# Reciprocals of the softmax sums by block transposition and a DRAM scratch, and a shorter head, in a fused attention and two-layer MoE kernel

## The chip, the cores and the metric

One core of a Trainium2 chip runs the whole program: masked attention and then two dense feed-forward layers. The metric is the device time of one execution in microseconds (us); it is compared as the median of several runs. The core's engines work side by side, each through its own instructions in order: TensorE (PE in the rows, its weight loads PEld), VectorE (DVE), ScalarE (ACT), GpSimd (POOL), and SyncE (SP), which here only issues DMAs. A queue is named with a q: SPq is what SyncE issues, ACTq what ScalarE issues.

## The reference

`q`, `k`, `v` are 2 x 8 heads of 768 x 64. Each row of q and of k gets a bucket from six sign bits of its product with `proj` (64 x 6). Attention is kept where the buckets agree:

```python
q_bits = (einsum('bhsd,dk->bhsk', q, proj) > 0); k_bits = (einsum('bhsd,dk->bhsk', k, proj) > 0)
mask = q_bucket[:, :, :, None] == k_bucket[:, :, None, :]
scores = where(mask, scale * q @ k.T, -1e9)
attn = exp(scores - max(scores)); attn = attn / (sum(attn) + 1e-9)
x = (attn @ v), laid out as 1536 tokens x 512
x = relu(x @ w_in) ** 2 @ w_out          # 512 -> 2048 -> 512
out = silu(x @ w_in2) @ w_out2           # 512 -> 2048 -> 512
```

All of it is in float32 quality: the kernel splits every operand in a high and a low part and makes three products.

## The kernel before, in words

The 16 heads are 8 pairs. A pair has 12 steps of its own (three blocks of 128 query rows for each of four half heads), so the attention is a loop over `d`, written out in order by hand: a prologue from d = -5, 96 steps, and a tail. One step `d` makes, on TensorE: six 128x128 transpositions of exponentials (`transp`, twice three), four products with v (`av`) of exponentials that are two steps older, and the four score products of a later block (`score_mm`). Its scores are read in the next step: VectorE takes the row maximum (`row_max`, `row_live`), ScalarE the exponential (`score_exp`). Each transposed tile is copied by ScalarE as high part (`t_hi`, tile `th`) and VectorE subtracts for the low part (`t_lo`, tile `tl`). The transposed tiles use three PSUM buffers in turn (`ps_t`), the scores two (`ps_s`): the second transposition of step d+2 takes the buffer that the first of step d+1 had, and so waits for that one's `t_lo`.

Once a pair there is a long step (d = 5, 17, 29, ... 77). In it TensorE also makes the sign bits of a later pair (`bits_mm`, 12 products), VectorE compares them (`bits_cmp`, two halves of 48x384, with a `t_lo` between), and two DMAs place the twelve rows of the pair's first head into the tiles that the scores are made of: `qq` by the SyncE queue, `kk` by the ScalarE queue (`place_bits`). ScalarE issues that DMA before the next step's `t_hi`, SyncE issues it behind the load of `vr` of the same step (`load_v`). The scores of step d+2 are the first that read these rows, in their third and fourth product (those with 76 rows). VectorE also does the early weight conversion in these steps (`w_exp`, `w_sign`, `w_low`): one such instruction in d = 29 and 77, two in 17, 41, 53 and 65.

The softmax sums of a pair (128 x 12) are turned into a tile of reciprocals spread over the columns of the transposed result: VectorE takes the reciprocal (`norm_rows`, d0+2 with d0 the step after the pair's last), GpSimd spreads it to 128x768, TensorE transposes that in six pieces (`rb_mm`, in the long step d0+5; for the seventh pair in step 92), ScalarE copies the result out of PSUM (`x_norm`; for the seventh pair VectorE multiplies), and GpSimd multiplies and stores (`x_mul`, `x_put`, one step later). The last pair goes its own way.

In the prologue the bits of the very first head are made with small products (`first_bits_mm`, `first_bits_cmp`), those of the second are placed by two DMAs (`second_place`). Products on zeros (`warm_up`; table `WARM`) are put between them.

The two MoE layers follow; their order comes from a planner with costs (`Plan`), and the change does not touch them.

Of the kernel before, what the change touches and what calls it, by code (L numbers as in the profile page):

```python
# [31 lines left out]
WARM = {-5: 3, -4: 2, -3: 2, -2: 2, 0: 1, 1: 1}  # L32
# [412 lines left out]
def lsh_attention_moe_moe(ctx, tc, kd, qk, qf, fq, v, pc, wi1, wo1, wi2, wo2, out):  # L445
# [22 lines left out]
    ps_o = att.enter_context(tc.tile_pool(name="ps_o", bufs=1, space=PSUM))  # L468

# [57 lines left out]
    def bits_mm(p):  # L527
        t = pair[p]
        hp, lp = t["hp"], t["lp"]
        ops = [(w[:, 48 * i : 48 * i + 48], x) for i in range(2) for (w, x) in ((pjh, hp[i]), (pjl, hp[i]), (pjh, lp[:, i]))]  # L530
        s = ps_s.tile([128, 2, 512], F32, tag="s", name=f"bs{p}")[:, 0], ps_t.tile([128, 512], F32, tag="t", name=f"bt{p}")
        for z in range(2):
            for j, (w, x) in enumerate(ops):
                mm(s[z][0:48, 0:QW], w, x[:, z * QW : (z + 1) * QW], start=j == 0, stop=j == 5)  # L534
# [86 lines left out]
    def first_bits_mm(i, z, warm=0):  # L621
        o = first["bits", i, z] = ps_t.tile([128, 512], F32, tag="t", name=f"bf{i}{z}")
        ops = first_ops(0, z)[i]
        for n, (w, rows_, x) in enumerate(ops):
            mm(o[0:76, 0:QW], pjd[rows_, w, 0:76], x, start=n == 0, stop=n == len(ops) - 1)  # L625
            if n == 0:
                warm_up(warm)

    def first_bits_cmp(i, z):
        m = tm[1 + i][64:76]  # L630
        nc.vector.tensor_scalar(
            out=pair[0][("qq", "kk")[i]][0][64:76, 1, half(z)], in0=first["bits", i, z][64:76, 0:QW],
# [185 lines left out]

    def norm_rows(p):
        ri = sums[p]  # L820
# [4 lines left out]
    rows = {}  # L825

    def rb_mm(p):
        s = ps_s.tile([128, 2, 512], F32, tag="s", name=f"rb{p}")
        for c in range(6):
            o = s[:, c // 3, c % 3 * 128 : c % 3 * 128 + 128]  # L830
            nc.tensor.transpose(o, rows[p][:, c].rearrange("p h d -> p (h d)"), ident)  # L831
        return s
# [6 lines left out]
    def x_norm(s, p):  # L839
        ta = xs[p][0].rearrange("p (a b) -> p a b", a=2)  # L840
        if p < 6:
            nc.scalar.copy(out=rows[p].rearrange("p c h d -> p (c h d)").rearrange("p (a b) -> p a b", a=2), in_=s[:, :, 0:QW])
        else:
            nc.vector.tensor_tensor(out=x_rows(p).rearrange("p (a b) -> p a b", a=2), in0=s[:, :, 0:QW], in1=ta, op=ALU.mult)

    def x_mul(p):
        if p < 6:
            ta = xs[p][0]
            nc.gpsimd.tensor_tensor(out=ta if p < 4 else x_rows(p), in0=rows[p].rearrange("p c h d -> p (c h d)"), in1=ta, op=ALU.mult)
# [20 lines left out]
    extra = defaultdict(list)  # L870
# [27 lines left out]
    for p in range(NPAIR):  # L898
        d0 = 12 * (p + 1)
        at(d0 + (-3 if p < NPAIR - 1 else -4), norm_sums, p)  # L900
        at(d0 + (2 if p < NPAIR - 1 else -3), norm_rows, p)
# [28 lines left out]
    with tc.manual_schedule():  # L930
# [12 lines left out]
        make_identity(nc, ident)  # L943

# [34 lines left out]
        at(-1, second_place)  # L979
# [20 lines left out]
        for d in range(-5, G // 2 + 3):  # L1000
# [25 lines left out]
            more = extra.pop(d, [])  # L1026
            if ready and more and d not in long:
                score_exp(*ready, m)
# [99 lines left out]
```

## Time and profile before

| | us |
|---|---|
| median of 3 runs (741.33 to 741.73) | 741.59 |
| the profiled execution | 741.74 |
| its span | 740.0 |
| attention, prologue and tail | about 0 to 236 |
| the two MoE layers | about 236 to 740 |

In the profile's page a line of the first part gives busy time, share of the span and instructions of every engine. In the timeline a row is: start, duration, engine, source line, operation, written tile and read tiles, shapes, how many were merged (x6), and in brackets how long the engine had been idle before and who ended that. Rows of the chain of work that ended last are: start, duration, engine, tile, line. Rows of a table of stretches are: the stretch, its length, then busy time and instructions of each engine, the granted TensorE clock (1.00 is full), the share of the 16 DMA engines, GB/s. The granted clock is 1.00 in every stretch of this profile.

### The profile page before, as it was taken

The page shows a single profiled execution, that of the slowest core. Times are in us where ns is not written, and L with a number is a line of the kernel's source. Part 1 is how long each engine was busy: PE and PEld are TensorE (multiplying, and loading weights), DVE is VectorE, ACT ScalarE, POOL GpSimd, SP SyncE. Part 2 cuts the span into 40 slices and gives each one's busy share as a digit, 9 for nine tenths or more (in the row PEclk, how much of TensorE's full clock was granted, in tenths as well). Part 3 has the DMA queues.
Part 4 walks back from the last instruction along what each step waited for, and adds up shares of the span by engine and source line. Part 5 has one row for each costly group of instructions (what it writes and reads, how often), then busy time and mean ns, then how long its engine had stood idle before and what let it go on. Part 6 is the DMA issues. An engine that isn't in the chain of part 4 may idle for free.

```text
span 740.0 us, 10899 instructions
## 1 busy us (share of the span) xinstructions
PE 734.0 (99%) x3740; PEld 627.7 (85%) x3740; DVE 610.2 (82%) x1151; ACT 461.8 (62%) x866; POOL 249.6 (34%) x219
## 2 busy tenths in 40 slices
PE   9999999999999999999999999999999999999998
PEld 4899999999998888888888888888888888888887
DVE  6999999999999998887878896788888777776442
ACT  6898998998896882773566278366335525623510
POOL 7457477877684104103103103500330320230000
PEclk9999999999999999999999999999999999999999
DMA  6886886786462113311320220002123024010012
GB/s 177 205 179 156 182 184 168 164 184 150 112 158 61 57 58 113 113 59 57 114 86 19 96 86 28 29 29 85 58 100 128 30 78 150 1 58 1 1 71 100
DMA packets 27639, 71.87 MB, mean 97 GB/s; under 512 B 4184, under 2 KB 9048, under 8 KB 27584
## 3 DMA queue, kind: packets, MB, share of 16 engines
q1 hardware_dynamic: 24824, 64.52, 31.5%
q0 software_dynamic: 2160, 5.90, 3.7%
q10 hardware_dynamic: 600, 0.75, 0.4%
q8 instruction: 30, 0.49, 0.3%
q14 instruction: 25, 0.20, 0.1%
HBM read 49.80 MB, written 3.15 MB: 72 GB/s over the span
## 4 chain that ended last, share of the span: by engine, by line
PE 98%; DVE 1%; ACT 0%; issue 0%; ACTq 0%; DVEq 0%
PE bank L341 35%; PE bank L260 21%; PE bank L231 12%; PE s L741 9%; PE t L777 8%; PE o L801 4%; PE o L802 4%; PE warm L732 1%; PE bs L534 1%; PE bt L534 1%; PE rb L831 1%; ACT P L761 0%; DVE tl L788 0%; PE bs L641 0%; PE bf L625 0%
## 5 line engine op out<-in xcount | busy, mean ns | idle before, releaser
L160 POOL TENSOR_TENSOR wp<-wt,wp 128x512 fp32r<-128x512 f32 x56 | 78.2, 1407 | 329.6 <-ACT wp L158 307.5
L260 PE MATMUL bank<-xb,wp 128*128 128x512 f32 x480 | 110.1, 389 | 0.0
L788 DVE TENSOR_TENSOR tl<-t,th 128x384 fp32r<-128x384 f32 x192 | 104.9, 548 | 2.4 <-ACT th L782 2.2
L260 PEld LDWEIGHTS bank<-xb,wp 128*128 128x128 f32 x480 | 90.1, 188 | 18.7
L761 ACT ACTIVATE P<-s,mt 128x768 f32<-128x768 f32 x96 | 95.6, 996 | 11.8 <-DVE mt L753 7.2
L748 DVE TENSOR_REDUCE mt<-s 128x1 f32<-128x768 f32 x96 | 91.4, 952 | 4.9 <-PE s L741 4.2
L741 PE MATMUL s<-kk,qq 76*128 76x384 f32 (+1 forms) x384 | 84.6, 341 | 0.3 <-ACT P L761 0.2
L782 ACT CAST th<-t 128x384 fp32r<-128x384 f32 x192 | 82.3, 484 | 3.9 <-PE t L777 2.8
L158 ACT CAST wp<-wt 128x512 fp32r<-128x512 f32 x56 | 34.2, 619 | 78.2 <-DVE wt L215 44.5
L231 PE MATMUL bank<-x0h,wp 128*128 128x512 f32 x256 | 80.2, 389 | 0.0
L777 PE MATMUL t<-ident,P 128*128 128x128 f32 x576 | 79.3, 273 | 0.9 <-DVE tl L788 0.9
L777 PEld LDWEIGHTS t<-ident,P 128*128 128x128 f32 x576 | 67.8, 140 | 6.0 <-DVE tl L788 1.3
L801 PE MATMUL o<-th,vv 128*128 128x384 f32 x192 | 72.5, 378 | 0.0
L265 DVE TENSOR_TENSOR ts<-bank,ts 128x512 f32<-128x512 f32 x80 | 54.4, 690 | 19.9 <-PE bank L260 17.2
L741 PEld LDWEIGHTS s<-kk,qq 76*128 76x128 f32 (+1 forms) x384 | 67.9, 188 | 2.2 <-ACT P L761 1.0
L802 PE MATMUL o<-tl,vv 128*128 128x384 f32 x192 | 64.5, 336 | 0.3 <-DVE tl L788 0.3
L245 ACT ACTIVATE ts<-bank 128x512 f32<-128x512 f32 x48 | 28.6, 596 | 49.3 <-PE bank L260 28.8
L231 PEld LDWEIGHTS bank<-x0h,wp 128*128 128x128 f32 x256 | 48.0, 188 | 10.0
L160 DVE TENSOR_TENSOR gql<-ts,gqh 128x512 fp32r<-128x512 f32 x64 | 43.8, 703 | 8.9 <-ACT gqh L158 8.9
L173 ACT ACTIVATE wt<-raw 128x512 f32<-128x512 f32 x58 | 38.1, 670 | 20.3 <-POOL wp L160 17.6
L341 PE MATMUL bank<-wol,gqh 128*128 128x512 f32 (+1 forms) x132 | 50.5, 383 | 0.0
L341 PE MATMUL bank<-woh,gql 128*128 128x512 f32 (+1 forms) x132 | 50.5, 383 | 0.0
(185 smaller groups left out, 1634.1 us busy)
## 6 DMA issues: line engine op xcount, KB each, us to landing
raw<-in_dram SPq DMA_DIRECT2D x64, 512.0 KB
kk<-in_dram POOLq DMA_DIRECT2D x15, 384.0 KB, 5.8
qq<-hq SPq DMA_DIRECT2D x28, 192.0 KB
vr<-in_dram SPq DMA_DIRECT2D x8, 384.0 KB
ta<-ob SPq DMA_DIRECT2D x31, 96.0 KB
tb<-ob SPq DMA_DIRECT2D x31, 96.0 KB
out_dram<-ts SPq DMA_DIRECT2D x11, 256.0 KB
rq<-in_dram SPq DMA_DIRECT2D x7, 384.0 KB
```

The costliest lines, as they stand in the source:

```text
L160: add(("DVE", "POOL")[pool], l, lambda: eng.tensor_tensor(out=lo(), in0=src(), in1=hi().bitcast(F32), op=ALU.subtract), (*rk, *hk), lk, po ...
L231: mm(bank[b], w[:, x, op, sl], t["x0"][y][:, kt], start=kt == 0 and j == 0, stop=kt == 3 and j == 2)
L260: mm(bank[b], w[:, p, op, k * 128 : k * 128 + 128], x[:, q, xop, k], start=first and k == 0 and j == 0, stop=k == 1 and j == 2, skip_group ...
L341: mm(bank[b][:, 0:wd], x, y, start=i == 0 and n == 0, stop=i == FB - 1 and n == 2)
L741: mm(s[:, n, 0:QW], t["qq"][h][0:kk, ab, c0 : c0 + 128], t["kk"][h][0:kk, ab, n * QW : (n + 1) * QW], start=ab == 0, stop=ab == 1)
L748: nc.vector.tensor_reduce(out=m[:, 0:1], in_=s[:, :, 0:QW], op=ALU.max, axis=AX.XY, negate=True)
L761: nc.scalar.activation(out=e.rearrange("p (a b) -> p a b", a=2), in_=s[:, :, 0:QW], func=AF.Exp, scale=m[:, 1:2], bias=m[:, 2:3], accum_ou ...
L777: nc.tensor.transpose(t[:, j * 128 : (j + 1) * 128], P[u, j][:, kt * 128 : (kt + 1) * 128], ident)
L782: nc.scalar.copy(out=th, in_=PT[g][0][:, 0:QW])
L788: nc.vector.tensor_tensor(out=tl, in0=t[:, 0:QW], in1=th.bitcast(F32), op=ALU.subtract)
L801: mm(o[:, 0:QW], vv, th, start=kt == 0, stop=False)
L802: mm(o[:, 0:QW], vv, tl, start=False, stop=kt == KT - 1)
```

## The change

The reciprocals no longer go over TensorE. VectorE takes the reciprocal into columns 0 to 11 of a 128x32 tile and transposes that in 32x32 blocks; four DMAs of 12 rows each, issued by SyncE, write the four blocks into a 12x128 scratch in DRAM; two DMAs, issued two steps later, read it back, spread over 64 partitions each; GpSimd multiplies two steps after that. `norm_rows` moves from d0+2 into the long step d0+5 (step 86 for the seventh pair), ahead of the weight conversion there; `x_mul` and `x_put` move from d0+6 to d0+9 (90 for the seventh). The bits of a pair go into one PSUM buffer of the scores and are compared by one instruction of 48x768, behind both `t_lo`. The last pair keeps the old way.

In the head the fillers change: one instead of four between the first bits, none instead of three, two and two in d = -5, -3 and -2, seven instead of two in d = -4. The first bits of q are compared for columns 0 to 127 first and for the rest last. The products for the second head's bits are put in another order, and its bits are placed by halves, each half as soon as it is compared.

```diff
-WARM = {-5: 3, -4: 2, -3: 2, -2: 2, 0: 1, 1: 1}
+WARM = {-4: 7, 0: 1, 1: 1}
...
+    dr = att.enter_context(tc.tile_pool(name="dr", bufs=2, space=bass.MemoryType.DRAM))
...
-        s = ps_s.tile([128, 2, 512], F32, tag="s", name=f"bs{p}")[:, 0], ps_t.tile([128, 512], F32, tag="t", name=f"bt{p}")
+        s = ps_s.tile([128, 2, 512], F32, tag="s", name=f"bs{p}")
...
-    def bits_cmp(s, p, z):
-        if z == 0:
-            pair[p]["bt"] = a1.tile([128, S], F32R, tag="bt", name=f"bt{p}")
+    def bits_cmp(s, p):
+        pair[p]["bt"] = a1.tile([128, S], F32R, tag="bt", name=f"bt{p}")
         nc.vector.tensor_scalar(
-            out=pair[p]["bt"][0:48, z * QW : (z + 1) * QW],
-            in0=s[z][0:48, 0:QW],
+            out=pair[p]["bt"][0:48].rearrange("p (a b) -> p a b", a=2),
+            in0=s[0:48, :, 0:QW],
...
-            if n == 0:
-                warm_up(warm)
-
-    def first_bits_cmp(i, z):
+            if i + z + n == 0:
+                warm_up(1)
+
+    def first_bits_cmp(i, z, a=0, b=QW):
...
-        ops = [(64 - NBR * i, *x) for i in range(2) for x in first_ops(1, z)[i]]
+        ops = [(64 - NBR * i, *first_ops(1, z)[i][n]) for i, n in ((0, 0), (1, 0), (1, 1), (0, 1))]
...
-    def second_place():
+    def second_place(z):
...
-                out=pair[0][x][1][64 : 64 + NBR, 1, :].bitcast(F32), in_=first["bt"][NBR * n : NBR * n + NBR].bitcast(F32)
+                out=pair[0][x][1][64 : 64 + NBR, 1, half(z)].bitcast(F32), in_=first["bt"][NBR * n : NBR * n + NBR, half(z)].bitcast(F32)
...
     def norm_rows(p):
+        if p < NPAIR - 1:
+            nc.vector.reciprocal(out=rc[:, 0:12], in_=sums[p])
+            nc.vector.transpose(out=rt, in_=rc)
+            ris[p] = dr.tile([12, 128], F32, tag="ri", name=f"ri{p}")
+            for b in range(4):
+                nc.sync.dma_start(out=ris[p][:, 32 * b : 32 * b + 32], in_=rt[32 * b : 32 * b + 12])
+            return
...
-    def rb_mm(p):
...
-            nc.tensor.transpose(o, rows[p][:, c].rearrange("p h d -> p (h d)"), ident)
...
+    def spread(p):
+        rows[p] = w = a1.tile([128, 6, 2, 64], F32, tag="rw", name=f"rw{p}")
+        w = w.rearrange("p c h d -> p (c h d)")
+        r = ris[p].rearrange("(h c) t -> h (c t)", h=2)
+        for h in range(2):
+            nc.sync.dma_start(out=w[64 * h : 64 * h + 64], in_=r[h : h + 1].broadcast_to([64, S]))
...
-            k = d0 + (5 if p < NPAIR - 2 else 8)
-            extra[k].append((rb_mm, x_norm, p))
-            at(k + 1, x_mul, p)
-            at(k + 1, x_put, p)
+            k = d0 + 5 if d0 + 5 in long else d0 + 2
+            mid[k].append((norm_rows, (p,)))
+            at(k + 2, spread, p)
+            at(k + 4, x_mul, p)
+            at(k + 4, x_put, p)
...
-        first_bits_mm(0, 0, 2)
-        warm_up(1)
-        first_bits_mm(1, 0)
-        warm_up(1)
-        first_bits_mm(1, 1)
         for i, z in ((0, 0), (1, 0), (1, 1)):
-            first_bits_cmp(i, z)
+            first_bits_mm(i, z)
+        for i, z, a, b in ((0, 0, 0, 128), (1, 0, 0, QW), (1, 1, 0, QW), (0, 0, 128, QW)):
+            first_bits_cmp(i, z, a, b)
...
-        at(-1, second_place)
+            mid[z - 2].append((second_place, (z,)))
...
-                bits_cmp(t, long[d], 0)
                 t_lo(g + 1)
-                bits_cmp(t, long[d], 1)
-            for dve, t, p in held:
-                dve(t, p)
-            if ready and not more and d not in long:
+                bits_cmp(t, long[d])
+            elif ready:
                 score_exp(*ready, m)
```

## Rows read from the trace of the kernel before

**Rows 1.** The page's first part: busy time of every engine.

```profile
PE 734.0 (99%) x3740; PEld 627.7 (85%) x3740; DVE 610.2 (82%) x1151; ACT 461.8 (62%) x866; POOL 249.6 (34%) x219
```

**Rows 2.** The timeline of TensorE from the long step 17 on.

```profile
59.47 0.82 PE L831 MATMUL rb<-ident,rw 128*128 128x128 f32 x6
60.05 0.94 PE L741 MATMUL s<-kk,qq 128*128 128x384 f32 x4
...
62.90 0.82 PE L777 MATMUL t<-ident,P 128*128 128x128 f32 x6
...
64.25 0.86 PE L741 MATMUL s<-kk,qq 128*128 128x384 f32 x4
64.95 0.27 PE L777 MATMUL t<-ident,P 128*128 128x128 f32 x1
```

**Rows 3.** The timeline of VectorE in the same stretch.

```profile
57.75 0.68 DVE L708 SCALAR_TENSOR_TENSOR wi<-raw,wi 128x512 uint32<-128x512 uint32 x1
...
58.69 0.55 DVE L788 TENSOR_TENSOR tl<-t,th 128x384 fp32r<-128x384 f32 x1
59.15 0.66 DVE L540 TENSOR_SCALAR bt<-bs,tmt 48x384 fp32r<-48x384 f32 x1
...
60.20 0.66 DVE L540 TENSOR_SCALAR bt<-bt,tmt 48x384 fp32r<-48x384 f32 x1
...
62.23 0.56 DVE L788 TENSOR_TENSOR tl<-t,th 128x384 fp32r<-128x384 f32 x1
```

**Rows 4.** The timeline of ScalarE there: the DMA of the bits.

```profile
60.90 0.73 ACTq L661 DMA_DIRECT2D kk<-bt  x1
```

**Rows 5.** The timeline of the long steps 53 and 29.

```profile
144.91 0.56 DVE L788 TENSOR_TENSOR tl<-t,th 128x384 fp32r<-128x384 f32 x1
...
145.42 0.38 PE L777 MATMUL t<-ident,P 128*128 128x128 f32 x2
...
88.45 0.96 DVE L748 TENSOR_REDUCE mt<-s 128x1 f32<-128x768 f32 x1 [0.50 <-PE s L741]
```

**Rows 6.** The timeline of the SyncE queue in and after step 17.

```profile
57.19 0.59 SPq L670 DMA_DIRECT2D vr<-in_dram  x1
60.89 0.78 SPq L661 DMA_DIRECT2D qq<-bt  x1
61.73 1.67 SPq L489 DMA_DIRECT2D rk<-in_dram  x1
```

**Rows 7.** The table of stretches while those bits travel (the last columns count).

```profile
62.75:63.25 0.50, 0.50 (x6) 0.47 (x5) 0.20 (x2) 0.50 (x1) 0.50 (x1) 1.00 0.26 43
63.25:63.75 0.50, 0.50 (x7) 0.50 (x6) 0.50 (x1) 0.50 (x3) 0.50 (x1) 1.00 0.00 0
```

**Rows 8.** The timeline of steps 86 to 94.

```profile
216.84 0.22 DVE L821 RECIPROCAL sums<-sums 128x12 f32<-128x12 f32 x1
...
229.22 0.95 DVE L844 TENSOR_TENSOR ys<-rb,ta 128x768 f32<-128x768 f32 x1
...
229.36 1.93 POOL L696 TENSOR_SCALAR wt<-wt 128x512 f32<-128x512 f32 x1 [1.09 <-ACT wt L692]
...
231.56 0.91 DVE L700 TENSOR_SCALAR wt<-wt 128x512 uint32<-128x512 uint32 x1
```

**Rows 9.** The chain of work that ended last, in the first 25 us.

```profile
1.31 4.02 PE warm L732 x9
...
13.54 1.01 PE bs L641 x4
14.55 0.54 PE warm L732 x2
```

**Rows 10.** The timeline of the head.

```profile
9.62 0.83 ACT L608 CAST qq<-fr 128x768 fp32r<-128x768 f32 x1
...
11.44 0.99 ACT L761 ACTIVATE P<-s,mt 128x768 f32<-128x768 f32 x1 [0.99 <-PE s L741]
...
12.57 0.96 PE L741 MATMUL s<-kk,qq 128*128 128x384 f32 x4
```

More of the change, by code (lines that the diff above doesn't have):

```diff
@@ L625, in first_bits_mm @@
             mm(o[0:76, 0:QW], pjd[rows_, w, 0:76], x, start=n == 0, stop=n == len(ops) - 1)
-            if n == 0:
-                warm_up(warm)
-    def first_bits_cmp(i, z):
+            if i + z + n == 0:
+                warm_up(1)
+    def first_bits_cmp(i, z, a=0, b=QW):
         m = tm[1 + i][64:76]
         nc.vector.tensor_scalar(
-            out=pair[0][("qq", "kk")[i]][0][64:76, 1, half(z)], in0=first["bits", i, z][64:76, 0:QW],
+            out=pair[0][("qq", "kk")[i]][0][64:76, 1, half(z)][:, a:b], in0=first["bits", i, z][64:76, a:b],
             scalar1=m[:, 0:1], scalar2=m[:, 1:2], op0=ALU.is_gt, op1=ALU.mult,
@@ L817, in norm_sums @@
         nc.gpsimd.tensor_scalar(out=sums[p], in0=sums[p], scalar1=1e-9, scalar2=None, op0=ALU.add)
+    rc = ac.tile([128, 32], F32, name="rc")
+    rt = ac.tile([128, 32], F32, name="rt")
     def norm_rows(p):
+        if p < NPAIR - 1:
[5 more added lines that the diff above has]
+            return
         ri = sums[p]
@@ L823, in norm_rows @@
         nc.gpsimd.tensor_copy(out=w, in_=ri.rearrange("p (h c) -> p c h", h=2).unsqueeze(3).broadcast_to([128, 6, 2, 64]))
-    rows = {}
-    def rb_mm(p):
-        s = ps_s.tile([128, 2, 512], F32, tag="s", name=f"rb{p}")
-        for c in range(6):
-            o = s[:, c // 3, c % 3 * 128 : c % 3 * 128 + 128]
-            nc.tensor.transpose(o, rows[p][:, c].rearrange("p h d -> p (h d)"), ident)
-        return s
+    rows, ris = {}, {}
+    def spread(p):
[4 more added lines that the diff above has]
+            nc.sync.dma_start(out=w[64 * h : 64 * h + 64], in_=r[h : h + 1].broadcast_to([64, S]))
     def x_sum(p):
@@ L837, in x_sum @@
             nc.gpsimd.tensor_tensor(out=ta[r, z], in0=ta[r, z], in1=tb[r, z], op=ALU.add)
[L839 to L844, printed above, removed]
     def x_mul(p):
-        if p < 6:
-            ta = xs[p][0]
-            nc.gpsimd.tensor_tensor(out=ta if p < 4 else x_rows(p), in0=rows[p].rearrange("p c h d -> p (c h d)"), in1=ta, op=ALU.mult)
+        ta = xs[p][0]
+        nc.gpsimd.tensor_tensor(out=ta if p < 4 else x_rows(p), in0=rows[p].rearrange("p c h d -> p (c h d)"), in1=ta, op=ALU.mult)
     def x_rows(p):
@@ L900, in lsh_attention_moe_moe @@
         at(d0 + (-3 if p < NPAIR - 1 else -4), norm_sums, p)
-        at(d0 + (2 if p < NPAIR - 1 else -3), norm_rows, p)
+        if p == NPAIR - 1:
+            at(d0 - 3, norm_rows, p)
         at(d0 + (3 if p < NPAIR - 1 else 0), x_sum, p)
         if p < NPAIR - 1:
-            k = d0 + (5 if p < NPAIR - 2 else 8)
-            extra[k].append((rb_mm, x_norm, p))
-            at(k + 1, x_mul, p)
-            at(k + 1, x_put, p)
+            k = d0 + 5 if d0 + 5 in long else d0 + 2
[3 more added lines that the diff above has]
+            at(k + 4, x_put, p)
     for i, (d_load, d_abs, *d_dve) in enumerate(W_STEPS):
@@ L1025, in lsh_attention_moe_moe @@
                 t_hi(g + 1)
-            more = extra.pop(d, [])
-            if ready and more and d not in long:
-                score_exp(*ready, m)
             if d in long:
@@ L1037, in lsh_attention_moe_moe @@
                 t = bits_mm(long[d])
-            held = [(dve, pe(p), p) for pe, dve, p in more]
             if d in long:
-                bits_cmp(t, long[d], 0)
                 t_lo(g + 1)
-                bits_cmp(t, long[d], 1)
-            for dve, t, p in held:
-                dve(t, p)
-            if ready and not more and d not in long:
+                bits_cmp(t, long[d])
+            elif ready:
                 score_exp(*ready, m)
@@ L1061, in lsh_attention_moe_moe @@
         assert not new
-        assert not todo and not extra and not mid and not scale
+        assert not todo and not mid and not scale
         att.close()
```

6 lines of the change are left out of this document (3 added, 3 removed).

## The prediction

> **What bounds the kernel now.** I read the page's first part, then the chain of work that ended last, then the timelines of single long steps engine by engine, last the DMA traffic. The page shows TensorE busy for 734.0 of 740.0 us and VectorE for 610.2 [rows 1]; a busy TensorE says little by itself, so what counts is whether its groups follow each other. In a long step they do: transpositions of the reciprocals at 59.47, scores at 60.05, and a plain step later everything again, 64.25 to 64.95 for a group of four scores [rows 2]. So TensorE sets the pace, and what is taken off it is time saved, as long as nobody else becomes late. VectorE and ScalarE are close behind, so the question is who comes next. The head up to some 20 us is another thing: there the chain alternates between waits for exponentials and fillers that stand in TensorE's queue [rows 9, 10]. Everything after 236 us only moves with it.
>
> **What TensorE loses.** The six transpositions of a pair cost it 60.05 - 59.47 = 0.58 us [rows 2]; six pairs have them in a long step: 3.48 us, and the seventh 0.58 in step 92. Two other queues decide how much of that arrives.
>
> **VectorE in the long step.** Before: from the first `t_lo` at 58.69 to the end of the second compare, 60.20 + 0.66 = 60.86, it is 2.17 us [rows 3]. After: two `t_lo` at 0.46 (59.15 - 58.69) and one compare of 768 columns. That form is not in the trace. A 768-column operation on PSUM takes 0.95, the 384-column `t_lo` 0.55 [rows 3, 8], so 384 more columns cost 0.40, and the compare 0.66 + 0.40 = 1.06. Sum 1.98, a saving of 0.19. Added ahead of the weight conversion: the reciprocal 0.22 [rows 8], its hand-over 0.03 (the compare ends at 60.86, the DMA that waits for it starts at 60.89 [rows 3, 6]), and the 128x32 block transposition, which no row shows: at least nothing, at most the 0.66 of a compare with twelve times the columns; I take 0.22, the reciprocal's, which has the same partitions and is as small. That is 0.47 added, 0.28 net (0.06 to 0.72): the bits are compared 0.28 later, at 61.14. The Trainium skill (VectorE: DVE Perf Modes, "The three transpose paths") gives 0.311 us for a 128x128 bf16 transposition in 32x32 blocks; this would put ours below that, and the sum would change by less than 0.1 a pair. No row here shows it.
>
> Behind the compare stands ScalarE: it waits for it to issue the DMA of the kk bits (60.90, 0.73 [rows 4]), only then comes `t_hi` of the next step, then `t_lo`, which ends at 62.23 + 0.56 = 62.79 [rows 3]. The second transposition of step 19 needs that buffer; it starts half a group after 62.90, at 62.90 + 0.29 = 63.19 [rows 2]. The slack is 0.40 us. If TensorE comes 0.58 earlier and `t_lo` 0.28 later, the slack is overdrawn by 0.46, and 0.12 of the 0.58 stays. In step 53 `t_lo` ends at 145.47 and the transposition starts at 145.71 [rows 5]: slack 0.24, gain -0.04. Steps 17 and 41 are like the first, 53 and 65 like the second. In 29 and 77, with one conversion less, VectorE idles 0.50 before its next reduction [rows 5], which takes the 0.28; there some 0.5 stays. Sum over six: 0.24 - 0.08 + 1.0 = 1.2 us instead of 3.48.
>
> **The SyncE queue in the long step.** The four stores to the scratch are queued on SyncE ahead of the load of `vr` and of the qq bits. They wait for the block transposition: reciprocal from 57.75 [rows 3], 0.22 + 0.03 + 0.22 + 0.03, so the first is issued at 58.25. A DMA of twelve rows holds SyncE 0.78 and the next follows at 0.84 (60.89, 61.73), the 128-row load 0.59 [rows 6]. I take 0.84 for a store of twelve rows; lower bound 0.65 (the 128-row one with its gap), upper bound twice 0.84, since the next row shows 1.67 [rows 6]. Then `vr` is issued at 58.25 + 3.36 = 61.61 instead of 57.19 and the qq bits at 62.26 instead of 60.89, 1.37 late. Before, the traffic of the bits is over in the stretch that ends at 63.25 and nothing moves in the next [rows 7]: 2.36 us from issue to arrival. After: 62.26 + 2.36 = 64.62. The score group that needs them started at 64.25 [rows 2], and only its third product reads them, at 64.25 + 0.35 = 64.60. So the arrival falls on the old time, and the 0.58 is waited away, gain -0.02 a pair; with 0.65 a store it is 0.76 earlier, and VectorE's account above decides. If the 384 KB of `vr`, now right ahead in the same queue, delay them, it is worse; 0.1 us there is 0.6 over six pairs.
>
> The two accounts don't add; the later wait decides. For the six pairs I take 0.2 us, between -2.4 (0.4 worse each) and 1.2. The kk bits go over ScalarE's queue and are not behind the stores.
>
> **What lies beside other work.** ScalarE loses a 768-column copy a pair: it is not the bound there, nothing. GpSimd loses the spreading and multiplies three steps later, behind which only weight pieces for 236 us and the next casts stand: nothing, as long as it doesn't run over into the next long step. The two spreading loads a pair move 384 KB more; what waits for them is that multiplication alone: nothing.
>
> **Steps 86 to 94.** The reciprocal was there (216.84 [rows 8]); new is the transposition, 0.25 with its hand-over, in a step with one `t_lo` behind it: -0.25. In step 92 VectorE loses the 0.95 at 229.22 and TensorE 0.58, but VectorE's w_exp at 231.56 waits for GpSimd's 229.36 + 1.93 = 231.29 in any case [rows 8], so only about 0.2 comes through. Together about 0 (-0.3 to 0.6).
>
> **The head.** The first exponential starts at 11.44 [rows 10]. Ahead of it TensorE does four fillers between the first bits, of which one stays, and the first compare of q is cut to a third; so the first scores come over 1 us earlier. But ScalarE is busy till 9.62 + 0.83 = 10.45 with the second head's loads [rows 10], so the exponential starts at 10.46: 0.98 gained, and the score at 12.57 that waits for it comes at 11.59. The seven fillers fit in the wait: at 0.27 (0.54 / 2 [rows 9]) they take 1.9 at most, and the wait is about 1.6, so up to 0.3 of them may stick out. In the next two rounds a filler pair of 0.54 behind 1.01 of bits [rows 9] falls away; with that gone the loop of exponential, score and reduction limits, and I count half, 0.27 a round. Sum 0.98 + 0.54 = 1.5 us; bounds 0.7 (0.98 less what sticks out) and 2.06 (both pairs whole). The placement by halves must be done before step 1's scores; the halves are issued as much earlier as the scores are.
>
> **Sum.** 1.5 + 0.2 + 0 = 1.7. 741.74 of the profiled execution gives 740.04; it lies 0.15 above the median of the runs, so 739.9. About 0.2% (1.48 us) is what a measurement of this kernel can tell from no change: 740.11 and 743.07 are the borders.
>
> **The rivals.**
> Everything comes through: the stores are issued in 0.65 or less and the transposition costs next to nothing, or the slack is larger than I read. Then 1.5 + 3.48 + 0.58 = 5.6: 736.0. For it speaks that TensorE has no gap in these steps now; against it the 0.40 and 0.24 of slack and the twelve-row row of 0.78.
>
> Slower, by the SyncE queue alone: the qq bits arrive late for the third score product. From 0.25 us a pair later than before, the head's gain is gone; from 0.5 on it is slower by more than 0.2%. With 1.0 us a store (between 0.84 and 1.67) they are 0.64 later still: -0.66 x 6 + 1.5 = -2.5: 744.1. For it: 0.02 of reserve, and `vr` right ahead; against it: the queue is otherwise empty then [rows 7].
>
> The head gives little: the first exponential hangs on something else that doesn't move, such as the loads. Then 0.3 at most: 741.4. The clock is the other way to it: it is granted at 1.00, the 2.4 GHz level, in every stretch shown [rows 7], with fillers at 0.27 after the start against 0.45 in the first nine [rows 9]. If it fell in the two rounds from 12.6 to 17 for want of fillers, 0.70 + 1.01 of products a round would double: 3.4 lost, 0.98 kept, 743.8. Against it: the gaps left there are below 1 us. The Trainium skill (TensorE: Matmul & The Clock Gate, "What's actually happening") says that an idle TensorE drops to the lower clock, which speaks against taking fillers out; the rows show no drop, since the fillers are there.
>
> **Chances.** Forecast, 42%: own range 738.6 to 741.2 (head 0.7 to 2.06, pairs -0.3 to 1.0); more of it below 740.11 than above, 25 against 17. All through, 22%, all faster. Queue, 19%, of it 15 beyond 743.07 and 4 within. Head or clock, 17%: 13 within, 4 slower. Faster 0.47, same 0.34, slower 0.19. The range goes to 736.0, half of the second case, and to 743.0, where most of the third is left out.
>
> **What would show it.** In the pairs: an idle time of TensorE of about 0.5 us ahead of the third score product two steps after a long step, ended by the DMA of the qq bits; if it is instead ahead of a transposition, ended by `t_lo`, VectorE's account decided; if neither is there, all comes through. The store's issue time should be near 0.8 on SyncE, the block transposition near 0.2, the 48x768 compare 1.06. In the head: the first exponential at 10.5, the third score group at 11.6, the steady state 1.5 us earlier. Wrong it would be by a cheap store, by a `vr` that holds the bits back, by a clock below 1.00 in the first 20 us, or by a GpSimd queue that is late for the next bits.

## The result, and the profile after

The changed kernel takes 750.97 us (median of 4 runs, 750.14 to 751.59); the kernel before, beside it on the same chip, 741.46. The ratio is 1.0125 (95% interval 1.0113 to 1.0137): slower by 9.5 us, where 739.9 was forecast and 743.0 was the upper end. The profiled execution took 750.92, its span is 749.1.

The page's first part hardly tells of it. TensorE is busy for 0.6 us more than before [rows 1], VectorE for 1.4 more. The changed kernel:

```profile
PE 734.6 (98%) x3692; PEld 627.2 (84%) x3693; DVE 611.6 (82%) x1151; ACT 456.6 (61%) x860; POOL 246.8 (33%) x214
```

So I compared the starts of the score groups, one a step, in both timelines. The changed kernel is ahead by 1.84 us after the head, by 2.59 at the scores of step 53 (139.96 instead of 142.55), and behind by 3.71 at those of step 57 (154.59 instead of 150.88). Four steps lost 6.3 us. Till the last scores it falls back to 4.24 behind, till the first product of the MoE layers to 7.73 (243.57 instead of 235.84), and till the end to 9.18 (750.92 instead of 741.74). Two places, then: steps 54 to 57, and the end of the attention with what follows it at once (4.9 us).

The head went as forecast. The timeline of the changed kernel there: the first exponential starts at 10.58 instead of 11.44, the third score group at 11.71 instead of 12.57 [rows 10].

```profile
10.58 0.99 ACT L761 ACTIVATE P<-s,mt 128x768 f32<-128x768 f32 x1
...
11.71 0.98 PE L741 MATMUL s<-kk,qq 128*128 128x384 f32 x4
```

The first place, in the timelines of GpSimd, SyncE, VectorE and TensorE of the changed kernel:

```profile
125.31 1.84 POOL L853 TENSOR_TENSOR ta<-rw,ta 128x768 f32<-128x768 f32 x1 [4.82 <-DMA rw<-ri]
...
140.63 2.27 POOL L849 TENSOR_TENSOR ta<-ta,tb 128x768 f32<-128x768 f32 x1
...
136.52 0.46 SPq L814 DMA_DIRECT2D ta<-ob  x1
142.93 0.46 SPq L814 DMA_DIRECT2D tb<-ob  x1
143.48 2.14 SPq L829 DMA_DIRECT2D ri<-rt  x4
...
146.13 0.80 SPq L661 DMA_DIRECT2D qq<-bt  x1
...
138.24 0.22 DVE L825 RECIPROCAL rc<-sums 128x12 f32<-128x12 f32 x1
138.49 0.21 DVE L826 STREAM_TRANSPOSE rt<-rc 128x32 f32<-128x32 f32 x1
...
139.55 1.67 DVE L708 SCALAR_TENSOR_TENSOR wt<-raw,wt 128x512 uint32<-128x512 uint32 x1
...
142.07 1.06 DVE L540 TENSOR_SCALAR bt<-bs,tmt 48x768 fp32r<-48x768 f32 x1
...
141.75 0.55 PE L777 MATMUL t<-ident,P 128*128 128x128 f32 x3 [0.58 <-DVE tl L788]
...
149.16 0.59 PE L741 MATMUL s<-kk,qq 76*128 76x384 f32 x2 [2.45 <-DMA qq<-bt]
...
151.23 1.48 PE L741 MATMUL s<-kk,qq 128*128 128x384 f32 x4
```

Read it backwards. TensorE waits 2.45 us at 149.16 for the qq bits. SyncE issues these at 146.13, 3.0 us after the compare ended (142.07 + 1.06), because it stood at the copy into `tb` from 136.98 to 142.93, and what had queued behind that copy, the four stores (2.14 us) and `vr`, still came first. That copy may not overwrite `tb` before GpSimd has summed it, and the sum runs from 140.63 to 142.90. GpSimd has worked without a gap above 0.1 us since 125.31; ahead of that it waited 4.82 us for the spread reciprocals to land. The table of GpSimd's waits, from 30 to 245 us, has that for all pairs: 35.4 us together, more than GpSimd waits for anything else there.

```profile
POOL ta L853 <- DMA rw<-ri: 20.4, 4, 7.0
POOL ys L853 <- DMA rw<-ri: 15.0, 3, 5.5
```

There is a second, shorter way from the late GpSimd to TensorE. VectorE's two weight pieces of this long step took 0.89 and 1.67 us, at 138.62 and 139.55, while GpSimd's late product and sum ran beside them. Over all the kernels here, 143 pieces of this form ran in the attention with no GpSimd instruction beside them, and they took 0.65 to 0.69. The low part and the compare stand behind these pieces, and TensorE waits 0.58 at 141.75 for the low part and 0.20 at 143.19 for the compare. With the multiplication later (below) neither wait is there.

The four steps from 139.96 took 3.23, 3.01, 5.03 and 3.36 us, where the kernel before took 2.05 to 2.17. In the last one nothing is waited for; the products are slow (four scores in 1.48 instead of 0.87). The table of stretches gives the granted clock (the 1.00 and 0.66 behind the engines): after the wait TensorE spends part of the stretch at the lower of its two levels, 1.2 GHz.

```profile
145.00:150.00 5.00, 2.43 (x15) 2.11 (x16) 2.25 (x7) 2.94 (x7) 4.97 (x5) 1.00 0.60 151
150.00:155.00 5.00, 5.00 (x25) 4.91 (x24) 3.92 (x10) 3.33 (x7) 2.56 (x2) 0.66 1.22 216
...
240.00:245.00 5.00, 5.00 (x16) 4.23 (x17) 4.80 (x8) 0.47 (x1) 3.47 (x3) 0.50 0.02 7
```

The second place, timelines of GpSimd, VectorE and TensorE of the changed kernel:

```profile
212.82 1.85 POOL L853 TENSOR_TENSOR ys<-rw,ta 128x768 f32<-128x768 f32 x1 [5.47 <-DMA rw<-ri]
...
234.06 1.83 POOL L853 TENSOR_TENSOR ys<-rw,ta 128x768 f32<-128x768 f32 x1 [4.83 <-DMA rw<-ri]
235.97 0.24 POOL L817 TENSOR_SCALAR sums<-sums 128x12 f32<-128x12 f32 x1
236.29 1.93 POOL L696 TENSOR_SCALAR wt<-wt 128x512 f32<-128x512 f32 x1
...
236.25 0.23 DVE L832 RECIPROCAL sums<-sums 128x12 f32<-128x12 f32 x1 [1.78 <-POOL sums L817]
...
239.79 0.69 PE L802 MATMUL o<-tl,vv 128*128 128x384 f32 x1 [2.23 <-DVE tl L788]
```

Here the sixth and the seventh pair's multiplications wait 5.47 and 4.83 us. The last sums and the weight limits stand behind them in GpSimd's queue, VectorE waits for these twice (1.78, shown, and 1.36 at 238.25), its low part is late, TensorE waits 2.23, and from 240 to 245 it runs at the lower level throughout (0.50). In the kernel before the same weight limit was at 229.36 [rows 8].

### The profile page after: what moved, and what is told of

Its sections match the earlier page's. It is cut to its first block, busy times and chain, and to the rows that moved or that the text cites. A ratio compares the mean times of both kernels' runs of the same rounds, so it can differ in the third digit from the quotient of the medians.

```text
span 749.1 us, 10848 instructions
## 1 busy us (share of the span) xinstructions
PE 734.6 (98%) x3692; PEld 627.2 (84%) x3693; DVE 611.6 (82%) x1151; ACT 456.6 (61%) x860; POOL 246.8 (33%) x214
## 2 busy tenths in 40 slices
DMA packets 29478, 74.65 MB, mean 100 GB/s; under 512 B 5104, under 2 KB 10016, under 8 KB 29424
## 4 chain that ended last, share of the span: by engine, by line
PE 78%; DVE 13%; DMA 4%; POOL 2%; ACT 1%; issue 1%; SPq 1%; DVEq 0%; ACTq 0%; POOLq 0%
PE bank L341 35%; PE bank L260 20%; PE bank L231 12%; DVE mt L748 5%; DVE tl L788 5%; PE s L741 3%; PE t L777 3%; DMA rw<-ri 2%; PE o L802 2%; PE o L801 1%; PE warm L732 1%; DMA qq<-lp 1%; DVE bt L540 1%; DVE mt L753 1%; ACT P L761 1%
## 5 line engine op out<-in xcount | busy, mean ns | idle before, releaser
L777 PE MATMUL t<-ident,P 128*128 128x128 f32 x576 | 81.4, 275 | 3.7 <-DVE tl L788 3.6
L341 PE MATMUL bank<-woh,gqh 128*128 128x512 f32 (+1 forms) x132 | 50.5, 383 | 0.0
```

The costliest lines, as they stand in the source:

```text
L341: mm(bank[b][:, 0:wd], x, y, start=i == 0 and n == 0, stop=i == FB - 1 and n == 2)
L777: nc.tensor.transpose(t[:, j * 128 : (j + 1) * 128], P[u, j][:, kt * 128 : (kt + 1) * 128], ident)
```

## The experiments: where the loss comes from

Theories: **GpSimd** (the multiplication waits in an in-order queue), **SyncE** (stores ahead of the bits), **VectorE** (more work ahead of the compare), **head** (fewer fillers). Numbers of before are always those of the same chip.

**The reciprocals alone, on the head of before.** The edit puts back the fillers, the first compares and `second_place` of before.

> The head of the kernel before with the reciprocals of the changed one. Theory GpSimd (the multiplication waits in GpSimd's queue for the landing of the two spreading loads, what stands behind it comes late, and that costs 6.3 us in steps 54 to 57 and about 5 us at the end of the attention): the head has nothing to do with the loss and its 1.84 us come on top, 752.8 (752.0 to 753.6). Theories SyncE (the four stores stand ahead of vr and the qq bits) and VectorE (more work ahead of the compare): the same 752.8, since both lie in the reciprocals too. Theory head (the loss comes from taking fillers out, through a lower clock): 741 to 743.

Measured: 752.83 (before 742.03), ratio 1.0137 (1.0109 to 1.0164). As expected by the first three; the head is not the cause.

**The multiplication two steps later.**

```diff
-            at(k + 4, x_mul, p)
-            at(k + 4, x_put, p)
+            n = 6 if p < NPAIR - 2 else 4
+            at(k + n, x_mul, p)
+            at(k + n, x_put, p)
```

> The changed kernel with the multiplication and the stores behind it two steps later (d0+11 instead of d0+9) for the first six pairs; the seventh is left alone. Theory GpSimd: the loads have landed when GpSimd gets there, the 6.3 us of steps 54 to 57 are not lost, the 5 us at the end are: 744.7 (743 to 746.5). Theories SyncE and VectorE: nothing that they speak of is moved, 751 (750 to 752).

Measured: 740.53 (before 742.03), ratio 0.9986 (0.9972 to 1.0). All of the loss is gone, the end's too, which I had expected to stay. The timeline of GpSimd shows why: the sixth pair's multiplication now waits 1.77, and the seventh's 4.99 us fall early enough that nobody waits behind it. The profiled execution took 742.77, near the top of this kernel's range (739.36 to 742.88); in it TensorE waits 1.41 and 0.98 us for the qq bits after the long steps 17 and 65.

```profile
209.87 1.84 POOL L853 TENSOR_TENSOR ys<-rw,ta 128x768 f32<-128x768 f32 x1 [1.77 <-DMA rw<-ri]
...
227.57 1.83 POOL L853 TENSOR_TENSOR ys<-rw,ta 128x768 f32<-128x768 f32 x1 [4.99 <-DMA rw<-ri]
```

**The multiplication without the spread.**

```diff
-        ... in0=rows[p].rearrange("p c h d -> p (c h d)"), in1=ta, op=ALU.mult)
+        ... in0=ta, in1=ta, op=ALU.mult)
```

> The changed kernel, but GpSimd multiplies the sum by itself instead of by the spread reciprocals, so the normalisation of seven pairs is left out; all DMAs, the reciprocals and the multiplication's place and length stay. Theory GpSimd: both losses go, 739.6 (738 to 742). Theories SyncE and VectorE: stores, compare and reciprocals are all there, 751 (750 to 752).

Measured: 741.18 (before 742.03), ratio 0.9989 (0.998 to 0.9999). With stores, loads and reciprocals in place and only the wait taken out, the loss is gone: SyncE and VectorE are not its cause by themselves.

**The stores behind vr and the bits.**

```diff
             mid[k].append((norm_rows, (p,)))
+            last[k].append((norm_store, (p,)))
```

> The changed kernel with the four stores of a long step issued by SyncE behind vr and the qq bits instead of ahead of them. Theory SyncE: the bits arrive as early as in the kernel before, the 6.3 us of steps 54 to 57 are not lost, 744.7 or less. Theory GpSimd: the queue's head is held by the copy into tb, which waits for the sum on GpSimd, and that stands ahead of all of these, so at most 1 us is gained: 750 (749.5 to 751.5). Theory VectorE: 751.

Measured: 748.52 (before 742.03), ratio 1.0087 (1.0065 to 1.011). Outside both ranges and between them: 6.5 us are left of the 9.5, so behind the held copy the stores cost about 3 us (1 to 5 by the two intervals; 3.5 in the traces at step 57, where this kernel is 0.25 behind instead of 3.71). The theory GpSimd had allowed them 1 us at most. SyncE's timeline of this kernel shows both. The copy into `tb` still stands till 143.02, and the bits follow 1.2 later instead of 3.2; TensorE's wait is 1.73 instead of 2.45. The profile names no releaser for it, but it ends 3.1 us after the issue of the bits, as in the changed kernel (3.0).

```profile
143.02 0.46 SPq L814 DMA_DIRECT2D tb<-ob  x1
...
144.21 0.78 SPq L661 DMA_DIRECT2D qq<-bt  x1
145.04 1.73 SPq L836 DMA_DIRECT2D ri<-rt  x4
...
147.29 0.59 PE L741 MATMUL s<-kk,qq 76*128 76x384 f32 x2 [1.73 <-issue]
```

**Two buffers for tb.** `("tb", 1)` becomes `("tb", 2)`, and `rc`, `rt` become columns of `pcr`.

> The changed kernel with two buffers for tb instead of one (room for it is made by putting the two small tiles of the reciprocals into columns of a tile that is done with by then; the fill with ones falls away, the columns transposed for nothing hold other finite numbers). The multiplication still waits in GpSimd's queue as before. Theory GpSimd through tb (GpSimd's lateness reaches TensorE because the sum is late, so the one tb is not free, so SyncE stands at the copy into tb with vr and the bits behind it): SyncE is not held, the 6.3 us of steps 54 to 57 are not lost, at the end some is: 743 to 746. Rival (lateness reaches TensorE by another way, such as VectorE slowed beside GpSimd or the casts of v): 749 to 751.

Measured: 743.6 (before 741.82), ratio 1.0022 (1.0013 to 1.0032), in the range of the theory. GpSimd still waits 28.3 us for the spread in this kernel, but SyncE's timeline has the copy into `tb` at 136.91 and the bits as soon as they are compared. The single `tb` is the main link between GpSimd and TensorE in steps 54 to 57. What is still lost there in this trace (2.67 ahead at step 52, 1.91 at step 57) goes the shorter way: the two weight pieces took 1.09 and 0.99 beside GpSimd. The profiled execution took 741.48, the lowest of ten, and shows no loss at the end of the attention (11.48 us from the last scores to the MoE layers); where the 1.8 us of the median lie is not shown.

```profile
136.91 0.59 SPq L814 DMA_DIRECT2D tb<-ob  x1
...
141.81 0.80 SPq L661 DMA_DIRECT2D qq<-bt  x1
```

**One pair's multiplication later**, `n = 6 if p == 2 else 4`, and another kernel with `p == 5`.

> The changed kernel, the multiplication two steps later for the third pair alone (step 47 instead of 45). After its wait of 4.8 us ahead of that multiplication GpSimd works without a gap for 27 us, and the late sum of the fourth pair, which holds tb, is in that stretch. Theory that this one wait makes the 6.3 us of steps 54 to 57: they go, the end's 5 us stay, 744.7 (743 to 746). Theory that the lateness adds up from pair to pair: at most a third of it goes, 749 or more.

> The changed kernel, the multiplication two steps later for the sixth pair alone (step 83 instead of 81). Theory that its wait of 5.5 us makes the end late (sum of the seventh pair, copy into tb, spreading loads, second wait of 4.8 us, then the last sums and the weight limits): the end's 5 us go, the 6.3 of steps 54 to 57 stay, 746 (745 to 747.5). Theory that the seventh pair's own wait makes it: 751.

Measured: 746.33, ratio 1.006 (1.0046 to 1.0075), for the third pair; 745.79, ratio 1.0057 (1.0044 to 1.007), for the sixth (before 741.55). In the third pair's trace the lead is 0.80 before the long step and 0.78 after step 57: that loss is gone. The median is 0.3 above the range. This execution has a lead of 1.60 at step 53 where the changed kernel had 2.59, and 0.8 of the 6.3 is the rise at step 53 itself, which is given back without any wait for GpSimd too (0.79 in the kernel without the spread). VectorE's weight piece ran with no GpSimd instruction beside it in that step:

```profile
140.31 0.69 DVE L708 SCALAR_TENSOR_TENSOR wt<-raw,wt 128x512 uint32<-128x512 uint32 x1
```

The same trace has a new loss in steps 78 to 80 (from 1.27 ahead at step 77 to 0.99 behind; the changed kernel loses 0.5 there), where the piece at 194.82 took 2.16 beside the sum at 194.56. In the sixth pair's trace steps 54 to 57 still cost 7.7 (from 2.59 ahead to 5.11 behind), and the stretch from the last scores to the MoE layers is no longer than before (11.45 us, before 11.6, in the changed kernel 15.1). Each place hangs on one pair's wait.

**One step later instead of two**, `n = 5`.

> The changed kernel, the multiplication one step later instead of two for the first six pairs: of the 4.4 to 4.8 us between issue and landing one step of 2.05 more lies ahead of it. Theory of a queue with some reserve: waits of 2 to 3 us are borne, 741 (740.3 to 742.5). Theory that every us of wait counts: about half of the 10 us that two steps gave, 745 to 746.

Measured: 740.63 (before 741.55), ratio 0.9988 (0.9979 to 0.9997). GpSimd bears the waits that are left (up to 3.4 us in the first four pairs, 4.7 in the last three): they cost nothing that can be measured, those of the changed kernel 10 us. The length of a wait alone doesn't decide. In the changed kernel the fourth pair's multiplication, at 159.67, waits longest, 7.04 us, and TensorE loses nothing by it: it is 3.72 behind at step 58 and 3.73 at step 76. What counts is what stands behind the wait, and when it is needed.

## The experiments: what the long step gives when GpSimd is out of the way

With the multiplication later, 1.0 to 1.5 us are left of the head's gain and nothing of six times 0.58. These kernels ask why.

**The head alone**, reciprocals as before.

> The kernel before with the head of the changed one, reciprocals as before. Theory that the head's gain arrives whole: 1.85 us at the seventh score and no wait afterwards gives it back, 739.9 with before at 741.75 (739.4 to 740.3). Rival: the long steps, which run without a gap before, are brought out of step and give part back: 740.5 to 741.2.

Measured: 740.25 (before 741.66), ratio 0.9984 (0.9975 to 0.9993): 1.2 to 1.4 us. In its trace the lead is 1.13 after the head and 1.06 at the last scores, so nothing is given back; this execution's head gained less than the 1.84 above. Over all kernels with this head it is 1.1 to 2.1.

**Multiplication later and stores last, both.**

> Both edits at once: the multiplication two steps later and the four stores behind vr and the qq bits. With the multiplication later, the qq bits still made TensorE wait 1.0 us once (step 44) and the low part of a transposed tile 1.4 us in three long steps. Theory that SyncE's stores are a second, smaller cause, after GpSimd's wait: 1.0 us less than with the multiplication later alone, 739.5 (738.9 to 740.2; before at 742.0 on that chip, so about 2.5 below before). Theory that the stores cost nothing of their own: 740.5, as with the multiplication later alone.

Measured: 740.58 (before 741.82), ratio 0.9984 (0.9975 to 0.9993). No more than the later multiplication alone: that the stores cost something of their own, once the multiplication is later, is not shown. The wait of 1.0 us at step 44 that the expectation names is not in the trace of the later multiplication; its waits for the bits are the two given above. The table of TensorE's waits of this kernel, from 17 us on:

```profile
PE t L777 <- DVE tl L788: 2.6, 5, 0.9
PE s L741 <- DMA kk<-bt: 0.9, 1, 0.9
```

The low part takes the place of the bits, by the chain of the prediction. In step 17 (timelines of ScalarE, VectorE and TensorE) ScalarE waits for the compare (58.60 to 59.66), issues the kk bits at 59.69, starts the high part at 60.52; the low part waits for that 0.20, the second transposition 0.30:

```profile
59.69 0.73 ACTq L661 DMA_DIRECT2D kk<-bt  x1
60.52 0.86 ACT L782 CAST th<-t 128x384 fp32r<-128x384 f32 x2 [2.20 <-DVE mt L748]
...
61.03 0.56 DVE L788 TENSOR_TENSOR tl<-t,th 128x384 fp32r<-128x384 f32 x1 [0.20 <-ACT th L782]
...
61.65 0.55 PE L777 MATMUL t<-ident,P 128*128 128x128 f32 x3 [0.30 <-DVE tl L788]
```

**The compare in halves again**, with the multiplication later: `bits_mm` and `bits_cmp` as before, a `t_lo` between.

> The multiplication two steps later, and the bits again in two PSUM tiles, compared in two halves with the low part between them, as in the kernel before. With the whole compare, TensorE waits 0.2 to 0.6 us for the low part in three of the long steps and steps after. Theory that the whole compare behind both low parts makes this: the waits shrink, 739.5. Theory that the reciprocal and the transposition ahead of it make it, and the whole compare with its 1.06 instead of 1.32 is a help: the same or up to 1.5 slower than the 740.5 of the multiplication later alone.

Measured: 741.71 (before 741.82), ratio 1.0006 (0.9996 to 1.0017). About 1.5 worse than whole, with intervals that overlap by a little: the one compare is no cause of the loss, rather a help.

**Reciprocal and transposition behind the compare.**

```diff
-            mid[k].append((norm_rows, (p,)))
+            (behind if k in long else mid)[k].append((norm_rows, (p,)))
...
                 bits_cmp(t, long[d])
+                for fn, a in behind.pop(d, []):
+                    fn(*a)
```

> The kernel with multiplication later and stores last, and the reciprocal and the transposition in a long step behind the compare instead of ahead of the weight conversion. Theory chain: the compare ends 0.43 earlier, so the high part too; the low part stands behind the same VectorE work and gains only the 0.2 that it waited for the high part: five times 0.2, 739.6. Rival, what counts is the work on VectorE in that step and not its order: 740.6.

Measured: 739.93 (before 741.66), ratio 0.9976 (0.9967 to 0.9985). 0.6 better than with both edits, a little less than the chain's five times 0.2; the intervals overlap, so the size is uncertain.

**The kk bits by SyncE.** `(nc.scalar if n and not h else nc.sync)` becomes `nc.sync`.

> The kernel with multiplication later and stores last, and the kk bits of a pair's first head issued by SyncE behind the qq bits instead of by ScalarE. There TensorE still waits 0.3 to 0.9 us for the low part of a transposed tile in five of the long steps and steps after, 2.6 us in all. Theory (chain of the prediction: whole compare, ScalarE's issue of the kk bits, high part, low part, transposition): ScalarE no longer waits for the compare, these waits shrink to less than half, 739.2 or less with 740.6 for the kernel with both edits. Rival, VectorE has no room left whatever stands ahead of it: the same waits, 740.6. Rival, the kk bits come 0.8 later on SyncE and are waited for: 741 or more.

Measured: 740.41 (before 741.66), ratio 0.9988 (0.9979 to 0.9997). No faster than with both edits (0.9984). Its table of TensorE's waits shows the chain cut, and another wait, for a DMA that also queues on SyncE, in its place:

```profile
PE s L741 <- DMA kk<-lp: 1.0, 1, 1.0
...
PE t L777 <- DVE tl L788: 0.3, 1, 0.3
```

**Both orders.**

> All four edits: multiplication two steps later, stores last, reciprocal and transposition behind the compare, kk bits by SyncE. Theory that the low part's wait and the order on VectorE were all that kept the 0.58 of each long step back: 738.0 (737.3 to 738.8 with before at 741.7). Rival, another wait takes their place (the kk bits or the low half of k, which then queue on SyncE): 739.9, no better than with the order on VectorE alone.

Measured: 740.88 (before 741.55), ratio 0.9993 (0.9983 to 1.0002); its runs lie between 739.2 and 743.1. The rival holds: TensorE waits 0.7 for the low half of k and 0.5 for the qq bits, and in the median nothing is won.

**The reciprocals early, out of the long step**: `norm_rows` at d0-1, `spread` at d0+1, `x_mul` at d0+6.

> The changed kernel with the reciprocals early: reciprocal, transposition and stores at step d0-1 (two steps after the last exponential of the pair, six ahead of the long step), the spreading loads at d0+1, the multiplication at d0+6 as in the kernel before (d0+5 for the seventh pair). Theory GpSimd first, SyncE and VectorE in the long step behind it: all three go, since five steps lie between load and multiplication and the long step holds no reciprocal and no store; the head's 1.84 and most of six times 0.58 arrive: 737.5 (736 to 739.5). Rival, VectorE's whole compare is what is late in the long step: the waits of 0.2 to 0.6 for the low part stay, 740. Rival, VectorE has no room for 0.43 us at d0-1: seven times 0.4 lost there, 740 to 741.

Measured: 743.23 (before 741.82), ratio 1.002 (1.0011 to 1.0029). Wrong, by the second rival and one more. The long steps do keep 0.33 to 0.43 each; the loss lies outside them. The plain step has no room: the lead falls by 0.35 from the scores of steps 11, 23, 35 and 47 to the next. And at step 59 the reciprocal itself waits for the sums, which GpSimd adds to behind its other work (timelines of VectorE and TensorE of this kernel):

```profile
155.05 0.23 DVE L825 RECIPROCAL rc<-sums 128x12 f32<-128x12 f32 x1 [1.35 <-POOL sums L817]
...
156.02 0.55 PE L777 MATMUL t<-ident,P 128*128 128x128 f32 x3 [1.56 <-DVE tl L788]
```

**No transposition on VectorE, one DMA that puts each element by itself.**

```diff
+        nc.sync.dma_start(out=ris[p].rearrange("c t -> t c"), in_=sums[p])
```

> The changed kernel without the block transposition: the reciprocal is taken at d0+2 as in the kernel before (at d0-1 for the seventh pair), and one DMA writes the 128x12 tile into the 12x128 scratch with every element put by itself, 1536 pieces of four bytes; spreading at d0+7, multiplication at d0+11 (d0+2 and d0+5 for the seventh). Theory that the 0.43 us on VectorE in the long step and what SyncE issues there are what is left of the loss: the waits for the low part and for the bits go, head and six times 0.5 arrive, 737.5 (736.5 to 738.5). Rival, 1536 pieces hold the DMA engines and other transfers come late: 741 or more. Rival, the whole compare alone keeps the low part late: 740.

Measured: 781.98 (before 741.66), ratio 1.0558 (1.0541 to 1.0575). TensorE waits 28.2 us for the kk bits, in six places, and the granted clock is 0.976 over the execution. The rival of the 1,536 pieces holds: from 56 to 64 us the DMA engines are busy for 0.92 and then 0.73 of the time while they move only 54 and 30 GB/s; between 64 and 68 us they are busy throughout (1.01) and TensorE for 0.69 of 4 us:

```profile
67.31 0.98 PE L741 MATMUL s<-kk,qq 76*128 76x384 f32 x2 [4.53 <-DMA kk<-bt]
...
64.00:68.00 4.00, 0.69 (x2) 0.71 (x3) 0.00 (x0) 0.02 (x1) 0.88 (x2) 0.78 1.01 216
```

**One store for the four**, on the kernel with reciprocal and transposition behind the compare; and the same with the kk bits by SyncE.

```diff
-        for b in range(4):
-            nc.sync.dma_start(out=ris[p][:, 32 * b : 32 * b + 32], in_=rt[32 * b : 32 * b + 12])
+        nc.sync.dma_start(out=ris[p].rearrange("c (b t) -> b c t", b=4), in_=rt)
```

> The kernel with multiplication later, stores last, reciprocal and transposition behind the compare, and one DMA that stores all four blocks (128 pieces of 128 bytes, into a 32x128 scratch of which twelve rows are used) instead of four of twelve rows. SyncE is held some 0.5 instead of 1.6 to 2.1 us there. Theory that SyncE's queue is what is left: 739.2 (738.6 to 739.7, before at 741.6). Rival, the waits left have nothing to do with SyncE: 739.9, as with four stores.

> The same with the kk bits issued by SyncE as well, so that ScalarE doesn't wait for the compare. Theory that SyncE's queue took back what this edit gave with four stores (740.9 there): now it comes through, 738.3 (737.5 to 739.2). Rival, the bits wait for something else than SyncE: 740 to 741, and executions 2 to 3 us apart as with four stores.

Measured (before 741.8): 739.84, ratio 0.9973 (0.9962 to 0.9984); with the kk bits by SyncE 738.66, ratio 0.9958 (0.9945 to 0.9971). One store by itself changes nothing, as its rival has it. With it the other edit comes through, as the theory of the queue has it: without it that edit gave 0.9993. This is the best version found, 0.42% below before. Its step 17, ScalarE and SyncE: the high part starts at 59.39 and waits for no compare; SyncE issues both bits and the store within 2.3 us.

```profile
59.39 0.86 ACT L782 CAST th<-t 128x384 fp32r<-128x384 f32 x2 [1.08 <-PE t L777]
...
59.40 0.78 SPq L661 DMA_DIRECT2D qq<-bt  x1
60.22 0.77 SPq L661 DMA_DIRECT2D kk<-bt  x1
61.09 0.58 SPq L835 DMA_DIRECT2D ri<-rt  x1
```

## Why the prediction was wrong, step by step

**The step that failed** is in the part on what lies beside other work. It priced GpSimd's later multiplication at nothing, "as long as it doesn't run over into the next long step", and the two spreading loads at nothing because what waits for them "is that multiplication alone". It counted the multiplication's 1.8 us and not the wait ahead of it, and with that wait GpSimd did run over: it was still busy at 140.63, in the long step 53. In an in-order queue whoever stands behind a waiting instruction waits too: casts, weight pieces, and the sum that frees `tb`, for which SyncE waits, behind which stand `vr` and the bits. From the first issue of the two loads to the multiplication's start it is 4.9 us in the first and 4.2 in the seventh pair (rows of SyncE and GpSimd below; the seventh multiplication is at 234.06, above) and 9.6 in the fourth, against the two steps, 4.1 us, that the change leaves, and the loads are issued at the end of a step, late when SyncE is. The trace of before has no such load, and I gave it no bounds. All this is shown by the later multiplication and by the multiplication without the spread; the link through `tb` by the second buffer. The shorter way, over VectorE's slower weight pieces, is read from the traces side by side and has no experiment of its own.

```profile
65.52 1.24 SPq L844 DMA_DIRECT2D rw<-ri  x2
...
70.43 1.83 POOL L853 TENSOR_TENSOR ta<-rw,ta 128x768 f32<-128x768 f32 x1 [4.41 <-DMA rw<-ri]
...
229.91 1.12 SPq L844 DMA_DIRECT2D rw<-ri  x2
```

**TensorE's 0.58 a pair**: right; at each long step's scores the lead grows by 0.55 to 0.79 and is then given back.

**VectorE's account**: right in its durations (0.22, 0.21, 1.06 for estimates of 0.22, 0.22, 1.06) and, where only it decides, in its result. In the kernel without the spread, steps 17, 53, 65 and 77 gain 0.14, -0.01, -0.02 and 0.42; forecast 0.12, -0.04, -0.04 and 0.5. Its chain through ScalarE's issue is shown by the kernel with the kk bits on SyncE.

**SyncE's account**: the store was mis-sized. Four took 1.55 to 2.14 us together in the changed kernel, 0.39 to 0.53 each, not 0.84. Yet in the kernel without the spread the bits were waited for 0.31 and 0.73 in steps 31 and 43, and the pairs of steps 29 and 41 give -0.34 and -0.86. The six pairs sum to -0.7 there, for a forecast of 0.2 (-2.4 to 1.2).

**Steps 86 to 94**: forecast about 0, without the spread -0.35 at step 87 and -0.2 by the MoE layers.

**The head**: 1.84 in the profiled execution, 1.2 to 1.4 alone by the medians, for a forecast of 1.5. Without GpSimd's wait the terms give 1.8 - 0.7 - 0.2 = 0.9 ahead, and that kernel measured 0.85 below before.

**The rivals.** "Slower by the SyncE queue" named the right wait, TensorE for the qq bits, with the wrong reason: its stores were cheaper than assumed, and what held the queue was the copy into `tb`; the stores made it worse by about 3 us of the 9.5. A small slip stands in the next one: 0.3 us off the median of 741.59 is 741.3, not 741.4. That the clock may fall was only weighed for the head, where it stayed at 1.00; it fell after the two long waits of TensorE. "A GpSimd queue that is late for the next bits" stood in the last sentence with no price and no rival.

**What stays open.** Runs of one kernel lie up to 4.8 us apart here (the kernel before, 741.33 to 746.09 in 23 runs; the compare in halves 4.4, both orders 3.9), and the profiles show a different DMA late by 0.3 to 1.4 in different kernels. Which one it is in which run, and why, was not settled; so single differences below 1 us between these kernels are not explained.

## What to carry to other kernels

A transfer that only one instruction off the critical path needs is not free: price the wait of that instruction's engine, list what stands behind it in the queue, and which single buffer that frees. Leave the load more time than its rows from issue to the reader's start show, or move the reader; here one step (2.05 us) was worth 10 us, and the next one nothing. When several small DMAs share a queue with an urgent one, make them one before anything else is moved onto that queue.

## What the runs showed of the hardware

The loads that spread 3 KB over 64 partitions each (192 KB, two a pair) needed 4.2 to 5.2 us from the first issue to the reader's start in six pairs of the changed kernel and 9.6 in the fourth; the reader waited for them each time. One DMA of 128 pieces of 128 bytes held SyncE 0.57 to 0.75 us, four of twelve pieces 1.55 to 2.14 in the changed kernel. Writing 1,536 elements of four bytes by one DMA, once for each of seven pairs, brought the packets from 29,478 to 39,671, and that kernel took 40 us more than the one before. The Trainium skill (DMA: Bandwidth & Descriptors, "Rules for kernel authors") says that a last dimension that isn't contiguous becomes one descriptor per element; the count of packets agrees, some 1,460 more a pair.

VectorE's weight piece took 1.67 us at 139.55, beside GpSimd's product of 1.63 at 139.04 and its sum of 2.27 at 140.63. Over all the kernels pieces of this form took 0.65 to 0.69 in the attention with no GpSimd instruction beside them, 0.88 to 2.16 where a cast, product or sum of GpSimd ran beside them for 0.3 us or more, and 0.67 to 0.68 beside the weight limit. The sum took 1.82 to 1.87 with no such piece beside it, and as much where it had started first (1.86 beside the piece of 2.16). No experiment moved the two apart with all else equal.
